# A tail rearranged in a fused top-k attention and MLP kernel: PE turns, a thinner MLP stretch, three products on GpSimd

## The chip, the cores and the metric

One core of one Trainium2 chip. The metric is the device time in microseconds (us) of one execution. Engines: PE (matmul), DVE (vector), ACT (scalar), POOL (GpSimd), SP (issues DMAs).

## What is computed

```python
scores = q @ k.T / 8                       # 8 batches x 8 heads, 576 x 576, head width 64
mask   = scores >= 32nd largest of the row
attn   = softmax of the masked scores
x      = (attn @ v), heads side by side    # 4608 x 512
h      = x @ w_in                          # 512 x 2048
out    = (max(h, 0) + alpha * min(h, 0)) @ w_out   # 4608 x 512
```

## The kernel before

**Tiles and ticks.** Two heads make a pair (32 pairs, `NPAIR`); a pair's score rows are nine tiles of 128 rows: tiles j = 0 to 7 are row chunk j // 2 of the head j % 2, and tile 8 holds the last 64 rows of both heads. The 288 tiles (`NT`) run in the list `ORDER`, one a tick of the loop at line 875. Every engine's order of work is written out by that loop; inside a tick, PE, ACT, DVE and POOL each get the steps of different tiles. `put(tick, slot, f)` files a step for a later tick, and `run(tick, slot)` issues what was filed. The slots "act", "pe", "dve", "dvx" and "end" stand at fixed places of the tick.

**One tile.** PE makes scores (`scores`, L333), ACT copies them with a bias (`act_b`, L342), sums their signs (`act_s`, L348) and takes the exponential (`act_e`, L353). POOL makes a sign word SG of the sum (`side_of`, L358), DVE flips the tile with it (`flip`, y, L364). One tick later DVE takes the eight largest of six segments (`seg_ops`, L374), then merges them (`merge_ops`, L389 and L391); every third tile the limit KP of the row is picked (L402 to L418). Seven ticks after the scores (`LAG_W`) the weights are made, in one of two ways: for tiles below `NW = NT - 6`, DVE makes a 0/1 mask (`mask`, L438, one buffer `mk`) and POOL multiplies it with the exponential (`weights`, L448); for the last six, DVE does both in one instruction (L445), at tick 289 for three and 292 for three. Each two tiles of a pair and chunk share a buffer `w2`, and SP issues a transposing DMA of it into `wT` (L461).

**The last batch.** The last four pairs, 28 to 31 (`LAST`, from `P0`), run chunk by chunk, so that a chunk's 128 output rows are ready for the MLP early. `tail_of` files for each chunk i and half g (two pairs): `av_last(i, g)` on PE (weights times v, 20 matmuls, L499, into `pu`), `rz_last` and `out_last` on DVE (reciprocal L568, scaled copy into `xb`, L575), `x_turn` (transposing DMA of `xb` into `xT`, L585) and the MLP block of these rows. For chunk three `turn_last` turns the rows with PE against an identity (L597) and copies them with DVE (L598).

**MLP.** `mlp_steps` gives a block's steps into a list `back`: ph steps (hidden rows, 16 matmuls of 128 columns, L725, followed by an ACT relu into gT, L731) and three pz steps (20 matmuls of 512 columns in parts of 7, 7 and 6, L739 and L743, followed by an ACT copy to o_sb, L748, and an output DMA). A block of 128 rows has four ph and three pz steps. Each tick the loop pops steps from `back` while `credit` (line 905) is above 0: 1.9 is added a tick, 2.4 from tick 288 on; a ph step costs 0.9, a pz part 1.5. Up to tick 253 one step a tick is popped, from tick 254 (`N0 + 2`) on as many as the credit allows. The ACT part of a popped step is issued at the start of the next tick. Matmul results of the MLP go to two PSUM banks in turn, from tick 288 on to the two score banks.

**The end.** `flush` empties `back`. Then `av_last(3, 1)`, `rz_last`, `out_last`, `last_ph(0)` (half of the hidden sums of chunk three, L611), `turn_last(1)`, `last_ph(1)` and `last_pz` (two halves of 256 columns, L628 and L631, copied by ACT and DVE, L634). `check_group` and `checks` (L466, L478 to L482) are sums over all tiles that end in a flag (`final_flag`, L486 and L487; `read_flag`), after which a slow general path is run or skipped; they are filed for ticks 292 to 297.

Of the kernel before, what the change touches and what calls it, by code (L numbers as in the profile page):

```python
# [32 lines left out]
def kernel(  # L33
# [406 lines left out]
    def weights(n, fused):  # L440
        p, j = ORDER[n]
        d, t = pairs[p], tiles.pop(n)
        dst = w_dst(n)
        if fused:
            nc.vector.scalar_tensor_tensor(out=dst, in0=t["b"], scalar=row_limit(n),  # L445
                                           in1=t["e"], op0=ALU.is_ge, op1=ALU.mult)
        else:
            nc.gpsimd.tensor_tensor(dst, t["mk"], t["e"], ALU.mult)  # L448
        if j == 8:
            d["wTm"] = prep.tile([128, 9, 128], BF16, name="wT", bufs=6)  # L450
            if fused:
                nc.vector.tensor_copy(d["wm"][:, S:640], d["wm"][:, 0:64])
            else:
                nc.gpsimd.tensor_tensor(d["wm"][:, S:640], t["mk"][:, 0:64], t["e"][:, 0:64],
                                        ALU.mult)
            nc.sync.dma_start_transpose(d["wTm"][:, 0:5, :], d["wm"])
            nc.sync.dma_start_transpose(d["wTm"][:, 5:9, :], d["wm"][:, 64:S])
        elif j % 2 == 1:
            wT = prep.tile([128, 9, 128], BF16, name="wT", bufs=6)
            d["wT", j // 2] = wT  # L460
            nc.sync.dma_start_transpose(wT, d["w2"])  # L461

    xb, xm = {}, {}

# [87 lines left out]

    pul = {}

    def av_last(i, g):
        x_tiles(B - 1)
        m = 128 if i < 4 else 64
        pul[i, g] = pu = ps_d.tile([128, 4, V1], FP32, name="pu", tag="pd")
        for s in range(2):
            d = pairs[P0 + 2 * g + s]  # L560
            for side in range(2):
                cs = slice(0, 128) if i < 4 else slice(64 * side, 64 * side + 64)
                av_one(pu[0:m, 2 * s + side, :], d, d["wT", i] if i < 4 else d["wTm"], side, cs)

    def rz_last(i, g):
        m = 128 if i < 4 else 64
        rz = attn.tile([128, 6], FP32, name="rz", bufs=4)
        nc.vector.reciprocal(rz[0:m, 0:4], pul[i, g][0:m, :, D])  # L568
        pul[i, g] = pul[i, g], rz

    def out_last(i, g):
        m = 128 if i < 4 else 64
        pu, rz = pul.pop((i, g))
        dst = xb[B - 1][i] if i < 4 else xm[B - 1]
        nc.vector.tensor_tensor(  # L575
            dst[:, 256 * g:256 * g + 256].rearrange("p (s d) -> p s d", s=4), pu[0:m, :, 0:D],
            rz[0:m, 0:4].unsqueeze(2).to_broadcast([m, 4, D]), ALU.mult)
# [11 lines left out]
    t7 = 7 * S  # L589
    CL = t7 % NX + 64 + 384  # L590

    def turn_last(h):
        pool, tag = (ps_a, "pa") if h == 0 else (ps_m, "misc")
        xa = pool.tile([128, 2, 128], BF16, name="xa", tag=tag)
        for j in range(2):
            c0 = 128 * (2 * h + j)
            nc.tensor.transpose(xa[:, j, :], xb[B - 1][3][:, c0:c0 + 128], ident_b)  # L597
        nc.vector.tensor_copy(xT[:, 2 * h:2 * h + 2, CL:CL + 128], xa)  # L598

    lastc = {}  # L600

# [17 lines left out]
                        lastc["ph"][u // 2][:, u % 2, :].rearrange("p (f t) -> p f t", f=4),  # L619
                        AF.Relu)  # L620

    def last_pz():
        o0 = t7 + 384
        for h, (pool, tag) in enumerate(((ps_a, "pa"), (ps_m, "misc"))):
            cs = slice(256 * h, 256 * h + 256)
            pz = pool.tile([128, 256], FP32, name="pz", tag=tag)
            for kk in range(NKT):
                nc.tensor.matmul(pz, xT[:, kk, CL:CL + 128], w_id_b[:, kk, cs], start=(kk == 0),  # L628
                                 stop=False)
            for f in range(NFT):  # L630
                nc.tensor.matmul(pz, lastc["g"][:, f, 0:128], w_out_b[:, f, cs], start=False,  # L631
                                 stop=(f == NFT - 1))
            o_sb = mlp.tile([128, DM], FP32, name="o_sb", tag="stage", bufs=3)
            (nc.scalar.copy if h == 0 else nc.vector.tensor_copy)(o_sb[:, 0:256], pz)  # L634
            nc.sync.dma_start(out[o0:o0 + 128, cs], o_sb[:, 0:256])

    def weight_steps():
        hold = {}
# [133 lines left out]

    PE_TICK = 1.9
    LAG_S, LAG_M, LAG_W = 2, 3, 7
    NW = NT - 6

    E = mybir.EngineType
    with tc.manual_schedule(engines={E.PE, E.Activation, E.DVE, E.Pool, E.SP}):
        cal = {}

        def put(tick, eng, f):
            cal.setdefault((tick, eng), []).append(f)

        def run(tick, eng):
            for f in cal.pop((tick, eng), ()):
                f()
# [8 lines left out]
            while blocks and blocks[0][0] + blocks[0][1] <= lim:  # L795
                back.extend(mlp_steps(*blocks.pop(0)))

        def flush():
            while back:
                pe_f, act_f, _, takes = back.popleft()  # L800
                if takes and len(after) >= 2:
                    after.popleft()()
                pe_f()
                if act_f:
                    after.append(act_f)
            while after:
                after.popleft()()

        def tail_of(n, wn):
            wp, wj = ORDER[wn]  # L810
            b = wp // KPB
            if wp in (PA, PA + 1):
                if (wj == 8 or wj % 2) and wp == PA + 1:
                    i = wj // 2
                    put(n + 3, "pe", lambda: av_alt(i))
                    put(n + 4, "dve", lambda: rz_alt(i))
                    put(n + 6, "act", lambda: out_alt(i))
                    put(n + 6, "end", lambda: x_turn(b, (i,)))
                    if i in (1, 3, 4):
                        lim = (b + 1) * S if i == 4 else b * S + 128 * i + 128  # L820
                        put(n + 9, "end", lambda: feed(lim))
            elif wp < P0:
                if wj == 3:
                    put(n + 3, "pe", lambda: av(wp, 0))
                    put(n + 4, "dve", lambda: av_rz(wp, 0))
                    put(n + 6, "act", lambda: av_out(wp, 0))
                    if wp % KPB == KPB - 1 and b >= 5:
                        put(n + 6, "end", lambda: x_turn(b, (0, 1)))
                        put(n + 8, "end", lambda: feed(b * S + 256))
                if wj == 8:  # L830
                    put(n + 4, "pe", lambda: av(wp, 1))
                    put(n + 5, "dve", lambda: av_rz(wp, 1))
                    put(n + 7, "act", lambda: av_out(wp, 1))
                    if wp % KPB == KPB - 1:
                        put(n + 7, "end", lambda: x_turn(b, range(2 if b >= 5 else 0, 5)))
                        put(n + 9, "end", lambda: feed((b + 1) * S))
            elif (wj == 8 or wj % 2) and wp % 2:
                i, g = wj // 2, (wp - P0) // 2
                dt = 2
                if i == 3 and g == 1:  # L840
                    put(n + dt, "pe", flush)
                put(n + dt, "pe", lambda: av_last(i, g))
                where = "end" if i == 3 and g == 0 else "dvx"
                put(n + dt + 1, where if where == "end" else "dve", lambda: rz_last(i, g))
                put(n + dt + 1, where, lambda: out_last(i, g))
                if i == 3:
                    if g == 1:
                        put(n + dt + 1, where, lambda: last_ph(0))
                    put(n + dt + 2 - g, where, lambda: turn_last(g))
                    if g == 1:  # L850
                        put(n + dt + 1, where, lambda: (last_ph(1), last_pz()))
                elif g == 1:
                    put(n + dt + 1, "dvx", lambda: x_turn(b, (i,)))
                    put(n + dt + 2, "end", lambda: back.extend(mlp_steps(*last.pop(i))))

# [19 lines left out]
        while n < end or back or after:  # L875
# [26 lines left out]
            if n >= 3 and n % 3 == 0 and n - 3 < NT:  # L902
                sel_a((n - 3) // 3)
            nb = 1 if n < N0 + 2 else 2
            credit = min(credit, 0.0) + (2.4 if n >= NT else 1.9)
            first = True
            while back and credit > 0.0 and (first or nb == 2):
                pe_f, act_f, cost, takes = back[0]
# [31 lines left out]
            for i in range(max(len(segs), len(merges), 2)):  # L940
                if i < len(segs):
                    segs[i]()
                if i < len(merges):
                    merges[i]()
            run(n, "dve")
            if 0 <= lm < NT and lm % 3 == 0:
                limit(lm // 3)
            if pick and n < NT:
# [4 lines left out]
            if pick:  # L953
                sel_pr(mn // 3)
                held = [lambda m=mn // 3: sel_sum(m)]
                if mn % TPP == TPP - 1:
                    put(n + 2, "dve" if mn < NT - 1 else "end", lambda g=mn // TPP: check_group(g))
                    if mn == NT - 1:
                        put(n + 2, "end", checks)
                        put(n + 3, "end", final_flag)  # L960
                        put(n + 7, "end", read_flag)
            run(n, "end")
            n += 1
        assert not cal and not blocks and not last
# [138 lines left out]
```

## Time and profile before

| what | value |
|---|---|
| median of three runs | 877.69 us (875.2 to 878.11) |
| profiled execution | 876.05 us |
| its span, first to last instruction | 873.9 us |
| mean granted TensorE clock | 0.925 |
| last DVE copy ends | 867.79 us |

Times inside the profile count from the span's start. Rows of the time order give start, duration, engine, line, operation, out <- in, the count that was merged, and in brackets the idle time before it with what ended it. Rows of the waits give the total, the number and the longest. Rows of the stretches give each engine's busy time with the count of its instructions, the granted clock, the DMA engines' share and GB/s.

### The profile page before, as it was taken

Reading aid. Unit: us, or ns where it says so; the run is one execution under the profiler, and the core shown is the slowest. Engines: PE = TensorE matmul, PEld = TensorE weight load, DVE = VectorE, ACT = ScalarE, POOL = GpSimd, SP = SyncE. Lnnn points to the kernel's source line nnn. Section 1 sums busy time; section 2 is a strip of 40 time slices with the busy share of each in tenths; the row PEclk is TensorE's granted clock in tenths of the full one; section 3 lists DMA queues with packets and bytes.
Section 4 is the critical chain, followed back from the end, with each engine's and each line's share of the span. In section 5 each row is a group of like instructions: output and inputs, shape, how many; then the busy total and the mean of one; then the engine's idle time right before and its main releaser. Section 6 shows DMA issues by size and latency. Waiting matters only on the chain. (4 is left out here: it accounts for less than half of the span.)

```text
span 873.9 us, 20604 instructions
## 1 busy us (share of the span) xinstructions
PE 715.2 (82%) x5698; PEld 425.6 (49%) x5771; DVE 834.9 (96%) x5187; ACT 789.7 (90%) x1872; POOL 430.3 (49%) x630
## 2 busy tenths in 40 slices
PE   5675698778968799777988789978897878999976
PEld 3443344334544345444454445644455555665655
DVE  4999999999999999999999999999999999899991
ACT  6999999989999999889999989999999998899841
POOL 1455445555555555555554545555555555455520
PEclk9568779889999999999997989999999999999989
DMA  7899645644665445564476446575455535444441
GB/s 161 159 171 211 120 90 89 129 90 95 134 144 109 101 108 113 103 135 94 108 158 123 85 97 130 108 135 96 96 123 120 120 71 124 92 90 97 77 95 45
DMA packets 342619, 99.37 MB, mean 114 GB/s; under 512 B 334672, under 2 KB 334944, under 8 KB 342496
## 3 DMA queue, kind: packets, MB, share of 16 engines
q1 hardware_dynamic: 340144, 95.58, 54.1%
q0 software_dynamic: 1152, 2.10, 1.8%
q8 instruction: 47, 0.77, 0.4%
q14 instruction: 76, 0.62, 0.2%
q10 hardware_dynamic: 1200, 0.30, 0.2%
HBM read 36.71 MB, written 9.44 MB: 53 GB/s over the span
## 5 line engine op out<-in xcount | busy, mean ns | idle before, releaser
L448 POOL TENSOR_TENSOR w<-mk,e 128x576 bf16<-128x576 bf16 x250 | 318.8, 1275 | 337.7 <-DVE mk L438 185.6
L374 DVE MAX8 C<-y 128x8 f32<-128x96 f32 x1728 | 418.4, 242 | 0.1
L333 PE MATMUL ps<-qkT 64*128 64x288 f32 (+1 forms) x1280 | 250.0, 468 | 28.3 <-ACT b L342 27.7
L348 ACT ACTIVATE h<-b 128x576 bf16<-128x576 f32 x288 | 203.5, 706 | 1.5
L342 ACT ACTIVATE b<-ps,NT 128x576 f32<-128x576 f32 x288 | 201.9, 760 | 1.9 <-PE ps L333 1.9
L725 PE MATMUL ph<-xT,w_in_b 128*128 128x128 bf16 (+2 forms) x997 | 151.2, 295 | 51.1 <-ACT gT L731 37.2
L353 ACT ACTIVATE e<-b 128x1152 bf16<-128x1152 f32 (+1 forms) x157 | 174.0, 1109 | 2.4 <-POOL w L448 2.3
L333 PEld LDWEIGHTS ps<-qkT 64*128 64x128 f32 (+1 forms) x1280 | 130.6, 192 | 89.5 <-ACT b L342 52.0
L389 DVE MAX8 L<-C 128x8 f32<-128x48 f32 x864 | 162.3, 188 | 0.1
L364 DVE TENSOR_SCALAR y<-b,SG 128x576 int32<-128x576 int32 x288 | 146.8, 510 | 9.0 <-POOL SG L358 8.5
L438 DVE TENSOR_SCALAR mk<-b,KP 128x576 bf16<-128x576 f32 x282 | 143.5, 509 | 0.0
L725 PEld LDWEIGHTS <-w_in_b 128*128 128x128 bf16 x1024 | 83.0, 102 | 113.1 <-issue 89.7
L743 PE MATMUL pz<-w_out_b,gT 128*128 128x512 bf16 x544 | 132.1, 380 | 1.1 <-issue 0.5
L731 ACT ACTIVATE gT<-ph 128x512 bf16<-128x512 f32 x140 | 85.9, 623 | 33.7 <-PE ph L725 33.5
L391 DVE MATCH_REPLACE8 C<-L,C 128x48 f32<-128x48 f32 x576 | 108.1, 188 | 0.0
L743 PEld LDWEIGHTS <-gT 128*128 128x128 bf16 x560 | 51.7, 98 | 68.4 <-issue 13.4
L499 PE MATMUL pu<-v_bf,wT 128*128 128x65 bf16 (+1 forms) x1600 | 68.6, 197 | 14.3 <-DMA wT<-w 7.3
L499 PEld LDWEIGHTS <-wT 128*128 128x128 bf16 (+1 forms) x1600 | 64.3, 102 | 25.7 <-DMA wT<-w 7.7
L358 POOL TENSOR_SCALAR SG<-S_all 128x1 int32<-128x1 f32 x288 | 64.7, 225 | 18.8 <-ACT h L348 18.8
L448 POOL TENSOR_TENSOR wm<-mk,e 128x576 bf16<-128x576 bf16 x32 | 40.8, 1275 | 50.3 <-DVE mk L438 46.2
L348 ACT ACTIVATION_READ_ACCUMULATOR h<-b 128x1 f32 x288 | 63.3, 220 | 0.0
L528 ACT ACTIVATE xb<-pu,rz 128x64 bf16<-128x64 f32 x208 | 50.6, 370 | 0.0
(116 smaller groups left out, 729.0 us busy)
## 6 DMA issues: line engine op xcount, KB each, us to landing
out_dram<-o_sb SPq DMA_DIRECT2D x34, 256.0 KB, 2.4
st_q<-in_q_dram SPq DMA_DIRECT2D x64, 128.0 KB, 2.9
st_v<-in_v_dram SPq DMA_DIRECT2D x64, 128.0 KB, 2.6
kst<-in_k_dram SPq DMA_DIRECT2D x62, 128.0 KB, 2.7
w_stage<-in_moe_w_out_dram SPq DMA_DIRECT2D x16, 256.0 KB, 3.1
w_in_b<-in_moe_w_in_dram POOLq DMA_DIRECT2D x8, 256.0 KB, 6.2
wT<-w SPq DMA_TRANSPOSE x128, 3.3
st_q<-in_q_dram SPq DMA_DIRECT2D x32, 32.0 KB, 2.5
```

What stands on the lines that cost most here:

```text
L333: nc.tensor.matmul(o_, l_, r_, start=True, stop=True)
L342: nc.scalar.activation(t["b"].rearrange("p (a c) -> p a c", a=2), t["ps"], AF.Identity, bias=NT0[:, p * TPP + j:p * TPP + j + 1], scale=ON ...
L348: nc.scalar.activation(h, tiles[n]["b"], AF.Sign, accum_out=S_all[:, n:n + 1])
L353: nc.scalar.activation(e, tiles[n0]["bu"], AF.Exp, scale=scl)
L364: nc.vector.tensor_scalar(t["y"].bitcast(I32), t["b"].bitcast(I32), FLIP, SG[:, n:n + 1], ALU.bitwise_xor, ALU.bitwise_xor)
L374: return [lambda g=g: nc.vector.max(out=C[:, n % TPP, g, :], in_=t["y"][:, g * SEG:(g + 1) * SEG]) for g in range(NSEG)]
L389: ops.append(lambda r=r, src=src: nc.vector.max(out=L[:, 8 * r:8 * r + 8], in_=src))
L438: nc.vector.tensor_scalar(t["mk"], t["b"], row_limit(n), None, ALU.is_ge)
L448: nc.gpsimd.tensor_tensor(dst, t["mk"], t["e"], ALU.mult)
L499: nc.tensor.matmul(o_, wT[:, 4 * side + c, cs], d["v"][:, 5 * side + c, :], start=(c == 0), stop=(c == 4))
L725: nc.tensor.matmul(hold[f][:, i, :], w_in_b[:, kk, (f + i) * 128:(f + i + 1) * 128], xT[:, kk, c0:c0 + tb], start=(kk == 0), stop=(kk == N ...
L743: nc.tensor.matmul(pz[0:m], hold["gT"][:, f, r0:r0 + m], w_out_b[:, f, :], start=False, stop=(f == NFT - 1))
```

## The change

- **Weights by PE.** For pair 31's chunk two and for chunk three of pairs 30 and 31 (`BY_PE`), the transposing DMA is left out. `w_turn` turns the nine 128-column blocks of `w2` with PE transposes in two parts (four and five), and ACT copies each part into `wT`. For chunk two it is issued in tick 287.
- **Chunk two's rows by PE.** `x_turn` of chunk two is left out. In tick 288, in a new slot "mid" (after DVE's merges, before KP and y), stand `rz_last(2, 1)`, `out_last(2, 1)`, four PE transposes and one ACT copy into `xT`, and the MLP block is filed there, in tick 288 instead of 290.
- **Less MLP work a tick.** From tick 254 to 265 the credit is 1.2 a tick instead of 1.9.
- **Three products on GpSimd.** `NW` is `NT - 3`: the tiles 282, 283 and 284 get mask and POOL product in ticks 289, 290 and 291; the last three stay with DVE in tick 292.
- **The finale** is one function in tick 292. It empties `back` down to two steps, turns weights, empties it to one, turns the rest, then runs `av_last(3, 1)` pair by pair with the turn of the first two 128-column blocks of chunk three's rows between, the last step of `back`, and the end as before.
- **Checks behind outputs.** `check_group` and `checks` are issued after `last_ph(1)`, `final_flag` after the first half of `last_pz`, `read_flag` after the second.

```diff
-        elif j % 2 == 1:
+        elif j % 2 == 1 and (p, j // 2) not in BY_PE:
...
+    BY_PE = ((NPAIR - 1, 2), (NPAIR - 2, 3), (NPAIR - 1, 3))
+
+    def w_turn(p, i, part):
+        d = pairs[p]
+        if part == 0:
+            d["wT", i] = prep.tile([128, 9, 128], BF16, name="wT", bufs=6)
+        cs = range(4 * part, 4 + 5 * part)
+        if i == 2:
+            pool, tag = ps_d, "pd"
+        else:
+            pool, tag = ((ps_a, "pa"), (ps_m, "misc"))[part]
+        wt = pool.tile([128, len(cs), 128], BF16, name="wt", tag=tag)
+        for c in cs:
+            nc.tensor.transpose(wt[:, c - cs[0], :], d["w2"][:, 128 * c:128 * c + 128], ident_b)
+        nc.scalar.copy(d["wT", i][:, cs[0]:cs[-1] + 1, :], wt)
...
-    NW = NT - 6
+    NW = NT - 3
...
-        def flush():
-            while back:
+        def flush(keep):
+            while len(back) > keep:
...
+        def finale():
+            pA, pB = NPAIR - 2, NPAIR - 1
+            flush(2)
+            w_turn(pA, 3, 0)
+            w_turn(pA, 3, 1)
+            w_turn(pB, 3, 0)
+            flush(1)
+            w_turn(pB, 3, 1)
+            rz_last(3, 0)
+            out_last(3, 0)
+            av_last(3, 1, (0,))
+            turn_pe(3, 0, 2, nc.scalar.copy)
+            av_last(3, 1, (1,))
+            rz_last(3, 1)
+            out_last(3, 1)
+            flush(0)
+            last_ph(0)
+            turn_pe(3, 2, 4, nc.vector.tensor_copy)
+            last_ph(1)
+            check_group(NPAIR - 1)
+            checks()
+            last_pz((final_flag, read_flag))
...
+                if (i, g) == (2, 1):
+                    put(n + 1, "pe", lambda: (w_turn(wp, i, 0), w_turn(wp, i, 1)))
+                    put(n + dt, "mid", lambda: (rz_last(i, g), out_last(i, g)))
+                    put(n + dt, "mid", lambda: turn_pe(i, 0, NKT, nc.scalar.copy))
+                    put(n + dt, "mid", lambda: back.extend(mlp_steps(*last.pop(i))))
+                    return
...
-            credit = min(credit, 0.0) + (2.4 if n >= NT else 1.9)
+            credit = min(credit, 0.0) + (2.4 if n >= NT else 1.2 if nb == 2 and n < N0 + 14 else 1.9)
```

More of the change, by code (lines that the diff above doesn't have):

```diff
@@ L553, with av_last @@
     pul = {}
-    def av_last(i, g):
+    def av_last(i, g, ss=range(2)):
         x_tiles(B - 1)
         m = 128 if i < 4 else 64
-        pul[i, g] = pu = ps_d.tile([128, 4, V1], FP32, name="pu", tag="pd")
-        for s in range(2):
+        if ss[0] == 0:
+            pul[i, g] = ps_d.tile([128, 4, V1], FP32, name="pu", tag="pd")
+        pu = pul[i, g]
+        for s in ss:
             d = pairs[P0 + 2 * g + s]
@@ L590, with turn_pe @@
     CL = t7 % NX + 64 + 384
[L592 to L598, printed above, removed]
+    def turn_pe(i, k0, k1, copy):
+        c0 = t7 % NX + 64 + 128 * i
+        pool, tag = (ps_a, "pa") if k0 == 0 else (ps_m, "misc")
+        xa = pool.tile([128, k1 - k0, 128], BF16, name="xa", tag=tag)
+        for k_ in range(k0, k1):
+            nc.tensor.transpose(xa[:, k_ - k0, :], xb[B - 1][i][:, 128 * k_:128 * k_ + 128],
+                                ident_b)
+        copy(xT[:, k0:k1, c0:c0 + 128], xa)
     lastc = {}
@@ L620, in last_ph, with last_pz @@
                         AF.Relu)
-    def last_pz():
+    def last_pz(between):
         o0 = t7 + 384
@@ L635, in last_pz @@
             nc.sync.dma_start(out[o0:o0 + 128, cs], o_sb[:, 0:256])
+            between[h]()
     def weight_steps():
@@ L839, in tail_of @@
                 dt = 2
-                if i == 3 and g == 1:
-                    put(n + dt, "pe", flush)
+                if (i, g) == (3, 1):
+                    finale()
+                    return
                 put(n + dt, "pe", lambda: av_last(i, g))
-                where = "end" if i == 3 and g == 0 else "dvx"
-                put(n + dt + 1, where if where == "end" else "dve", lambda: rz_last(i, g))
-                put(n + dt + 1, where, lambda: out_last(i, g))
                 if i == 3:
[L847 to L852, printed above, removed]
+                    return
+                if (i, g) == (2, 1):
[3 more added lines that the diff above has]
+                    put(n + dt, "mid", lambda: back.extend(mlp_steps(*last.pop(i))))
+                    return
+                put(n + dt + 1, "dve", lambda: rz_last(i, g))
+                put(n + dt + 1, "dvx", lambda: out_last(i, g))
+                if g == 1:
                     put(n + dt + 1, "dvx", lambda: x_turn(b, (i,)))
@@ L945 @@
             run(n, "dve")
+            run(n, "mid")
             if 0 <= lm < NT and lm % 3 == 0:
@@ L955 @@
                 held = [lambda m=mn // 3: sel_sum(m)]
[L956 to L961, printed above, removed]
+                if mn % TPP == TPP - 1 and mn < NT - 1:
+                    put(n + 2, "dve", lambda g=mn // TPP: check_group(g))
             run(n, "end")
```

## The prediction, before the changed kernel ran

> **What bounds the kernel now.** I read the page first, then the stretches of the last sixth, the waits there, and the time order of the end. All times are microseconds of the profiled execution, measured from its span's start.
>
> ```profile
> PE 715.2 (82%) x5698; PEld 425.6 (49%) x5771; DVE 834.9 (96%) x5187; ACT 789.7 (90%) x1872; POOL 430.3 (49%) x630
> ```
>
> DVE bounds the program, so an edit elsewhere counts only where DVE stands still. All edits lie behind tick 254, so I cut the rest of the span into stretches (PE, PEld, DVE, ACT, POOL busy; granted clock; DMA):
>
> ```profile
> 740.00:777.50 37.50, 35.30 (x331) 23.59 (x332) 34.28 (x212) 31.58 (x75) 18.53 (x27) 0.96 0.45 88
> 777.50:842.90 65.40, 60.46 (x583) 40.26 (x588) 65.14 (x394) 56.53 (x112) 34.54 (x49) 1.00 0.44 86
> 842.90:846.34 3.44, 0.00 (x1) 0.00 (x1) 3.44 (x15) 0.00 (x0) 0.00 (x0) 0.85 0.87 204
> 846.34:867.80 21.46, 20.50 (x233) 17.23 (x233) 8.88 (x37) 5.41 (x10) 0.00 (x0) 0.87 0.27 60
> 867.80:873.90 6.10, 0.00 (x0) 0.00 (x0) 0.00 (x0) 0.00 (x0) 0.00 (x0) 0.89 0.09 31
> ```
>
> DVE is idle for 3.22 in the first stretch, full in the second, and from 846.34 on PE is the bound: 20.50 of 21.46. The waits say why (us in total, times, longest; windows 740 to 845 for DVE, 735 to 785 for ACT, 740 to 874 for PE):
>
> ```profile
> DVE y L364 <- POOL SG L358: 2.7, 3, 1.8
> DVE rz L542 <- PE pu L499: 0.3, 1, 0.3
> ```
> ```profile
> ACT o_sb L748 <- PE pz L743: 4.2, 2, 3.4
> ```
> ```profile
> PE ph L725 <- DMA xT<-xb: 5.5, 2, 4.7
> ```
>
> The three stalls of `flip` are a chain: ACT stood 3.4 for the third part of an MLP product, so its sign sums came late, so SG, so `y`. The 4.7 of PE is chunk two's transposing DMA: the back list had run dry in ticks 289 and 290.
>
> **Less MLP work in ticks 254 to 265.** By the order of the instructions of both kernels: before, ticks 256 and 257 pop pz pz and pz, and the copy of that product stands ahead of tick 258's score copies on ACT. After, the same ticks pop ph and pz, and the copy stands at tick 260. Two product steps, about 3.0 by the rates below, lie ahead of the scores no more; the ACT wait was 3.4. I let all 3.0 of DVE stalls go (2.7 + 0.3; bounds 2.0 and 3.2). The price: five steps (two ph, three pz) pass behind tick 289. Ticks 266 to 287 pop 17 ph and 18 pz in place of 20 and 14. With the rates of the next fence (0.94 and 1.44) that is 3.0 more PE work in the second stretch, where PE had 65.40 - 60.46 = 4.9 idle. It fits, barely; the bound above is a new DVE stall of 1.5, as tick 275 now holds two pz besides its scores.
>
> **The end, walked through in the old time frame.** First the rates, from a part where PE ran at full clock:
>
> ```profile
> 820.00 3.75 PE L725 MATMUL ph<-xT,w_in_b 128*128 128x128 bf16 x64
> ...
> 825.24 1.02 PE L739 MATMUL pz<-w_id_b,xT 128*128 128x512 bf16 x3
> ...
> 829.56 0.80 PE L499 MATMUL pu<-v_bf,wT 128*128 128x65 bf16 x20
> 830.29 1.24 PE L333 MATMUL ps<-qkT 64*128 64x288 f32 x8
> ...
> 840.83 0.80 PE L499 MATMUL pu<-v_bf,wT 128*128 128x65 bf16 x20
> 846.34 3.57 PE L725 MATMUL ph<-xT,w_in_b 128*128 128x128 bf16 x32 [4.71 <-DMA xT<-xb]
> 849.70 1.30 PE L499 MATMUL pu<-v_bf,wT 128*128 128x65 bf16 x20
> 850.82 2.57 PE L725 MATMUL ph<-xT,w_in_b 128*128 128x128 bf16 x32
> 853.23 1.03 PE L739 MATMUL pz<-w_id_b,xT 128*128 128x512 bf16 x3
> ```
>
> A ph step of 16 takes 3.75 / 4 = 0.94; a product of 20 takes 829.56 - 825.24 = 4.32, so 1.51, 1.51 and 1.30 in its parts; a pu of 20 takes 0.73. A PE transpose has the shape of a ph matmul, so 0.06 each.
>
> Now DVE, ACT and POOL around it:
>
> ```profile
> 839.68 0.51 DVE L438 TENSOR_SCALAR mk<-b,KP 128x576 bf16<-128x576 f32 x1
> ...
> 841.89 0.14 DVE L418 SCALAR_TENSOR_TENSOR KP<-KK,SG 128x3 int32<-128x3 int32 x1
> ...
> 842.38 0.17 DVE L568 RECIPROCAL rz<-pu 128x4 f32<-128x4 f32 x1
> 842.59 0.42 DVE L575 TENSOR_TENSOR xb<-pu,rz 128x256 bf16<-128x256 f32 x1
> 842.93 2.27 DVE L445 SCALAR_TENSOR_TENSOR w<-b,KP,e 128x576 bf16<-128x576 f32 x3
> ...
> 848.97 2.28 DVE L445 SCALAR_TENSOR_TENSOR w<-b,KP,e 128x576 bf16<-128x576 f32 x3
> ```
> ```profile
> 834.97 1.09 ACT L731 ACTIVATE gT<-ph 128x512 bf16<-128x512 f32 x2
> ```
> ```profile
> 749.41 0.71 ACT L208 CAST v_bf<-st_v 128x640 bf16<-128x640 f32 x1
> ```
> ```profile
> 840.28 1.27 POOL L448 TENSOR_TENSOR w<-mk,e 128x576 bf16<-128x576 bf16 x1 [1.26 <-DVE mk L438]
> ```
>
> *Three products on GpSimd.* Three fused products (2.27) become three masks. Each mask takes about 0.45 of DVE's time (0.51, overlapped), so DVE is done some 0.9 earlier, near 850.3 instead of 851.25. One `mk` buffer makes each mask wait for POOL's 1.27, but at least 1.7 of other DVE work lies between them. This gain I cost at nothing: PE, not DVE, sets the end. If PE were early it would be worth its 0.9.
>
> *Chunk two by PE.* `rz_last(2, 1)` and `out_last` now run ahead of KP and `y`: from 841.89, done 842.01 + 0.51 = 842.52 (843.01 before). PE, which has done two ph and pu by about 841, waits for them. Then the last two transposes (0.2 with the hand-over), the ACT copy (half of 1.09: 0.5), and behind it on ACT the relu of the first ph (0.5), which PE's third ph needs for its bank: PE goes on at 843.8 instead of 846.34. So PE still stands some 1.3 to 2 ahead of `xb` and 1.1 behind it; the transposing DMA is out of the way. The first nine weight transposes, of pair 31's chunk two, sit in that slack and cost nothing; without it they would cost 0.55.
>
> *From 843.8, in program order on PE:* two ph 1.9, a product 4.3 (850.0); three ph 2.8, pu 0.7, a ph 0.9 (854.5); part one of the last block's product 1.5 (856.0); nine transposes 0.55, then 0.3 of waiting for the first ACT copy, four transposes 0.25 (857.1); part two 1.5, five transposes 0.3 (858.9); half of pu, two row transposes, the rest of pu after ACT's 640-wide copy 0.95 (859.85); part three 1.3 (861.15); `last_ph(0)` 1.8 (862.95). The rest is the old end:
>
> ```profile
> 860.30 0.28 PE L597 MATMUL xa<-ident_b,xb 128*128 128x128 bf16 x2
> ```
> ```profile
> 860.62 0.29 DVE L598 COPY xT<-xa 128x256 bf16<-128x256 bf16 x1 [1.26 <-PE xa L597]
> ```
> ```profile
> 860.96 1.95 PE L611 MATMUL ph<-xT,w_in_b 128*128 128x128 bf16 x32 [0.38 <-DVE xT L598]
> ```
> ```profile
> 867.37 0.42 DVE L634 COPY o_sb<-pz 128x256 f32<-128x256 f32 x1 [6.46 <-PE pz L631]
> ```
>
> ```profile
> wT<-w SPq DMA_TRANSPOSE x128, 3.3
> ```
>
> From 860.30 to 867.79 are 7.5, so after ends at 870.4 in the old frame against 867.8: **2.6 later**. It does 7.7 more PE work behind 843.8 (two ph, a product, weight turns with their waits 1.5); it starts 2.5 earlier and is spared the slow rows above (3.57, 1.30 and 2.57 for 1.9, 0.7 and 1.9). Weights of chunk three by PE save no wait here: DVE is done at 850.3, and a transposing DMA, 3.3 from issue to landing, would be there before PE asks at 856. They cost about 1.4 (bounds 0 and 2.6: a pair of transposes reads 0.28).
>
> *Checks behind outputs* move some 2.4 of DVE work under `last_ph(1)` and the products, where DVE has 6.46 idle: nothing, both ways. The 6.1 after the last copy stay.
>
> **The clock** is what I cannot walk through. Windows of 3.41, on the grid on which the granted clock changes:
>
> ```profile
> 736.07:739.49 3.42, 1.38 (x11) 0.76 (x10) 3.42 (x21) 3.39 (x8) 1.65 (x3) 1.00 0.98 159
> 739.49:742.90 3.41, 3.41 (x35) 3.35 (x32) 3.41 (x20) 2.06 (x7) 1.47 (x2) 0.50 0.24 71
> 804.34:807.75 3.41, 2.42 (x32) 1.55 (x28) 3.41 (x23) 3.41 (x8) 1.75 (x3) 1.00 0.52 142
> 841.89:845.30 3.41, 0.00 (x0) 0.00 (x0) 3.38 (x10) 0.00 (x0) 0.00 (x0) 1.00 0.79 189
> 845.30:848.71 3.41, 2.37 (x23) 2.37 (x23) 3.20 (x23) 0.41 (x1) 0.00 (x0) 0.50 0.54 102
> 848.71:852.13 3.42, 3.42 (x45) 3.42 (x43) 3.31 (x9) 0.78 (x2) 0.00 (x0) 0.50 0.35 66
> ```
>
> A window with PE busy 1.38 of 3.42 was followed by half clock; one with 2.42 was not. After has 2.4 to 3.1 of PE idle within some 3.5: most likely one window falls to half, which costs half of 3.41, 1.7 (bounds 0 and 3.4). The Trainium skill, "TensorE: Matmul & The Clock Gate", section "Part 1: The HAM clock gate", lets the clock fall only after at least one idle window of about 3.4 us. By that rule the clock holds here and the sum is 1.7 less; the trace speaks against it (1.38 busy was enough to fall), so it is a rival.
>
> **The sum.** -3.0 (stalls) + 2.6 (end) + 1.7 (clock) = +1.3. The profiled execution took 876.05 (span 873.9 and 2.15 around it), so 877.35 against it. It lies 1.64 below the median shown, 877.69; on that scale the forecast is **879.0**, no change that a measurement of this kernel can tell (about 0.3%, 2.6 us, so 875.1 to 880.3).
>
> **Rivals.**
> - *The clock holds*, because the wait is shared by two windows that each stay busy enough: -0.4, 877.3. For it: 2.42 busy held. Against: the row of 1.38. The Trainium skill's rule named above gives the same time.
> - *Slower: the half clock stays a second window.* Place: the two windows behind chunk two's wait. The rows of 845.30 and 848.71 show it after 2.37 busy at half clock. Another 1.7: 880.7. It decides when the PE wait straddles a window's edge, so that the first slow window is itself part idle. With a new stall of 1.5 from the fuller ticks it is 882.2.
> - *Faster: the end is shorter than walked.* The clock holds, 3.2 of stalls go, and the weight turns fit into waits that my walk doesn't have (ACT's relus ahead of PE in the finale), so their 1.4 cost nothing and the 0.9 of GpSimd counts: -3.2 + 2.6 - 1.4 - 0.9 = -2.9, 874.8. For it: the design of the finale, which only pays if PE gets there when DVE does. Against: PE's 20.50 of 21.46.
> - *The change doesn't do what it says:* ACT is late in ticks 254 to 265 all the same, since two row-8 score groups fall there, and only 2.0 of stalls go: 880.0.
>
> **How the numbers follow.** Forecast 0.29, clock holds 0.14, too few stalls removed 0.04: together 0.47 within 0.3%. Second slow window 0.25 and with new stalls 0.10: 0.35 slower by more. Shorter end: 0.18 faster by more. The range leaves out the outer half of the faster case and the worst of the slower one: 874.3 to 882.5.
>
> **What would show it.** Right: DVE without SG waits between 740 and 780 and everything there 3 earlier; the wait of ph for the DMA gone, one for ACT's relu of 1 in its place; PE busy through to the end; weight transposes far behind DVE's last product. Wrong: SG waits left or new ones after tick 266 (step one); PE waiting for DVE's last products in the finale, which would make the GpSimd edit count (step of the walk); the clock at full, or at half for over 3.41, behind chunk two.

## The result and the profile after

In paired runs the changed kernel took 879.49 us (median of 22, 876.16 to 882.03) and the kernel before 876.38 (22, 874.83 to 881.31). The ratio of these runs is 1.0027, 95% interval 1.0015 to 1.004: about 2.4 us slower (1.3 to 3.5; the medians alone stand 3.1 apart). That is inside the 0.3% that the prediction calls no change, but close to its edge of 2.6, and with so many runs the interval tells it from zero. The profiled execution took 878.3 us (span 876.4, granted clock 0.912) against 876.05 (873.9, 0.925).

The whole-span line of the page answers little: PE has 5.8 more, DVE the same.

```profile
PE 721.0 (82%) x5728; PEld 428.9 (49%) x5802; DVE 834.8 (95%) x5186; ACT 793.9 (91%) x1880; POOL 434.9 (50%) x633
```

The same stretches as before say more (PE, PEld, DVE, ACT, POOL busy; granted clock; DMA), with the end cut at DVE's last copy:

```profile
740.00:777.50 37.50, 33.95 (x326) 22.96 (x327) 36.90 (x228) 35.47 (x86) 20.01 (x30) 0.95 0.52 91
777.50:842.90 65.40, 59.45 (x570) 38.91 (x574) 65.14 (x394) 54.08 (x108) 34.31 (x48) 0.99 0.39 85
...
846.34:870.00 23.66, 22.08 (x265) 16.86 (x265) 6.83 (x22) 8.63 (x16) 0.43 (x1) 1.00 0.13 39
```

The first stretch shows the gain: DVE is busy 36.90 where it was busy 34.28. The third shows the loss: from 846.34 PE works 22.08, where it worked 20.50. The waits name both (DVE 740 to 845; PE 735 to 876):

```profile
DVE P L251 <- PE pr L243: 0.4, 1, 0.4
```
```profile
PE xa L615 <- DVE xb L593: 2.8, 1, 2.8
PE ph L745 <- ACT gT L751: 2.8, 4, 1.2
```

No SG wait is left on DVE (a new wait of 0.4, for PE's `pr`, is), and the 4.7 of `ph` for the DMA is gone. In its place the PE transposes of chunk two's rows wait 2.8 for DVE's `xb`, and the ph step behind them, the third of its block, 1.2 for ACT's relu. PE's time order (L615 row transposes, L745 ph, L759 and L763 pz, L476 weight transposes):

```profile
836.64 0.81 PE L515 MATMUL pu<-v_bf,wT 128*128 128x65 bf16 x20
837.28 0.27 PE L615 MATMUL xa<-ident_b,xb 128*128 128x128 bf16 x2
840.35 0.29 PE L615 MATMUL xa<-ident_b,xb 128*128 128x128 bf16 x2 [2.80 <-DVE xb L593]
841.81 3.33 PE L745 MATMUL ph<-xT,w_in_b 128*128 128x128 bf16 x32 [1.17 <-ACT gT L751]
...
855.03 0.67 PE L476 MATMUL wt<-ident_b,w 128*128 128x128 bf16 x9
856.09 0.38 PE L476 MATMUL wt<-ident_b,w 128*128 128x128 bf16 x4 [0.40 <-ACT wT L477]
```

The wait of 1.17 comes about in the same way, on ACT. ACT waited for the turned rows, while the relus of two ph steps that PE had finished at 836.8 came behind them in its program:

```profile
840.68 0.59 ACT L617 COPY xT<-xa 128x512 bf16<-128x512 bf16 x1 [3.72 <-PE xa L615]
```

After the wait the 32 ph matmuls take 3.33, where full clock takes 1.95. The windows of the clock's grid show why: PE was busy 0.29 of one, and the next ran at half.

```profile
837.92:841.33 3.41, 0.29 (x2) 0.17 (x3) 3.38 (x22) 0.65 (x2) 1.46 (x2) 1.00 0.57 123
841.33:844.75 3.42, 2.94 (x28) 2.94 (x28) 3.25 (x23) 1.52 (x3) 2.55 (x2) 0.50 0.24 45
844.75:848.16 3.41, 3.36 (x20) 1.70 (x20) 3.34 (x6) 0.60 (x1) 1.27 (x1) 1.00 0.46 89
```

DVE, in time order, with the anchors used below (mask of tick 288, `xb` of chunk two, the last fused products, the last copy):

```profile
837.45 0.52 DVE L438 TENSOR_SCALAR mk<-b,KP 128x576 bf16<-128x576 f32 x1
...
839.87 0.42 DVE L593 TENSOR_TENSOR xb<-pu,rz 128x256 bf16<-128x256 f32 x1
...
845.52 1.26 DVE L418 SCALAR_TENSOR_TENSOR KP<-KK,SG 128x3 int32<-128x3 int32 x1
846.82 2.27 DVE L445 SCALAR_TENSOR_TENSOR w<-b,KP,e 128x576 bf16<-128x576 f32 x3
...
859.45 0.18 DVE L586 RECIPROCAL rz<-pu 128x4 f32<-128x4 f32 x1 [5.98 <-PE pu L515]
...
869.62 0.42 DVE L653 COPY o_sb<-pz 128x256 f32<-128x256 f32 x1 [2.20 <-PE pz L650]
```

The two spans compare as follows. The mask of tick 288 comes 2.23 earlier (839.68 to 837.45), the last copy ends 32.59 behind it in place of 28.11, 4.48 more, and 6.36 follow in place of 6.11. Together 2.5, the difference of the spans.

### The profile page after: what moved, and what is told of

Same layout as the page of the kernel before. It is cut to its first block, busy times and chain, and to the rows that moved or that the text cites. A ratio compares the mean times of both kernels' runs of the same rounds, so it can differ in the third digit from the quotient of the medians.

```text
span 876.4 us, 20675 instructions
## 1 busy us (share of the span) xinstructions
PE 721.0 (82%) x5728; PEld 428.9 (49%) x5802; DVE 834.8 (95%) x5186; ACT 793.9 (91%) x1880; POOL 434.9 (50%) x633
## 5 line engine op out<-in xcount | busy, mean ns | idle before, releaser
L448 POOL TENSOR_TENSOR w<-mk,e 128x576 bf16<-128x576 bf16 x253 | 323.1, 1277 | 338.9 <-DVE mk L438 178.8
L374 DVE MAX8 C<-y 128x8 f32<-128x96 f32 x1728 | 421.0, 244 | 0.1
L745 PE MATMUL ph<-xT,w_in_b 128*128 128x128 bf16 (+2 forms) x997 | 152.6, 295 | 45.8 <-ACT gT L751 37.4
L438 DVE TENSOR_SCALAR mk<-b,KP 128x576 bf16<-128x576 f32 x285 | 145.3, 510 | 0.0
L745 PEld LDWEIGHTS <-w_in_b 128*128 128x128 bf16 x1024 | 81.8, 101 | 109.3 <-issue 85.9
L763 PE MATMUL pz<-w_out_b,gT 128*128 128x512 bf16 x543 | 132.1, 380 | 1.2 <-issue 0.5
L763 PEld LDWEIGHTS <-gT 128*128 128x128 bf16 x560 | 51.7, 98 | 68.0 <-issue 13.3
L515 PE MATMUL pu<-v_bf,wT 128*128 128x65 bf16 (+1 forms) x1600 | 70.8, 200 | 14.7 <-DMA wT<-w 8.9
L515 PEld LDWEIGHTS <-wT 128*128 128x128 bf16 (+1 forms) x1600 | 66.1, 104 | 25.5 <-DMA wT<-w 9.5
```

The source lines that it names most:

```text
L374: return [lambda g=g: nc.vector.max(out=C[:, n % TPP, g, :], in_=t["y"][:, g * SEG:(g + 1) * SEG]) for g in range(NSEG)]
L438: nc.vector.tensor_scalar(t["mk"], t["b"], row_limit(n), None, ALU.is_ge)
L515: nc.tensor.matmul(o_, wT[:, 4 * side + c, cs], d["v"][:, 5 * side + c, :], start=(c == 0), stop=(c == 4))
L745: nc.tensor.matmul(hold[f][:, i, :], w_in_b[:, kk, (f + i) * 128:(f + i + 1) * 128], xT[:, kk, c0:c0 + tb], start=(kk == 0), stop=(kk == N ...
L763: nc.tensor.matmul(pz[0:m], hold["gT"][:, f, r0:r0 + m], w_out_b[:, f, :], start=False, stop=(f == NFT - 1))
```

## The experiments

**Theory:** PE sets the end from chunk two on, and two edits that each pay spoil one another. The 1.2 credit frees DVE, but pushes MLP steps behind tick 289; the row turns of chunk two stand in PE's program ahead of these steps, so PE waits for `xb` with runnable work queued behind. **Rivals:** the weight turns of chunk three are the loss, the GpSimd edit is, or the clock alone. Each ratio is to runs of the kernel before that were made beside it (medians 876.11 to 877.44). A figure in us behind a ratio is a difference of ratios times 876.4. The last column is a length inside one profiled execution, from the start of DVE's `xb` of chunk two to the start of its last copy: it leaves out what happened earlier. `xb` itself stands 0.5 earlier where PE turns chunk two's rows (2.42 behind the mask of tick 288 in after, 2.91 in before), so compare this length among before, e1, e6 and e7, or among the others.

| kernel | median us | ratio to before, 95% | profile: `xb` to last copy |
|---|---|---|---|
| before | 876.38 | 1 | 24.8 |
| after | 879.49 | 1.0027 (1.0015 to 1.004) | 29.75 |
| e1: before, credit edit alone | 872.18 | 0.9944 (0.9932 to 0.9957) | 23.9 |
| e2: after, rows turned two ticks later | 874.23 | 0.9967 (0.9946 to 0.9988) | 25.4 |
| e3: after, chunk three's weights by DMA | 877.37 | 1.0005 (0.9992 to 1.0018) | 27.8 |
| e4: after, credit 1.9 again | 874.1 | 0.9974 (0.9962 to 0.9985) | 22.2 |
| e5: after, six fused products again | 879.7 | 1.0032 (1.0016 to 1.0048) | 30.6 |
| e6: e1 and checks behind outputs | 871.89 | 0.9945 (0.9923 to 0.9966) | 22.8 |
| e7: e6 and three products on GpSimd | 872.39 | 0.9954 (0.9934 to 0.9974) | 23.9 |
| e8: after, PE kept busy in the wait | 877.43 | 1.0006 (0.9989 to 1.0024) | 28.4 |
| e9: e2 and e3 together | 873.16 | 0.9959 (0.9939 to 0.9979) | 24.4 |

### e1: the credit edit alone

```diff
 (before)
-            credit = min(credit, 0.0) + (2.4 if n >= NT else 1.9)
+            credit = min(credit, 0.0) + (2.4 if n >= NT else 1.2 if nb == 2 and n < N0 + 14 else 1.9)
```

> The kernel before with one edit: credit 1.2 in ticks 254 to 265. Theory (PE paces the end; after loses by PE's wait for xb, the half clock behind it and the weight turns): the SG stalls of 740 to 780 go (2.7 less), the five deferred steps fill PE's 4.7 wait for the transposing DMA down to about 1, and no window falls to half clock: 4 to 5 us less than before, ratio about 0.995. Rival (the deferred MLP steps themselves make the end late, wherever the turns are made): the deferred 6.3 us of PE work come back at the end and eat the stalls: ratio 0.998 to 1.003.

It measured 0.9944, 4.9 us faster (3.8 to 6.0), as the theory had it. DVE's waits (740 to 845), then PE's time order in e1:

```profile
DVE P L251 <- PE pr L243: 0.6, 1, 0.6
```
```profile
837.61 1.95 PE L725 MATMUL ph<-xT,w_in_b 128*128 128x128 bf16 x32
839.39 1.03 PE L739 MATMUL pz<-w_id_b,xT 128*128 128x512 bf16 x4
840.25 3.62 PE L743 MATMUL pz<-w_out_b,gT 128*128 128x512 bf16 x16
...
851.86 0.19 PE L486 MATMUL ptot<-ones_f,tot 128*1 128x1 f32 x2 [1.42 <-DVE junkg L482]
```

The stalls are gone, and the steps pushed back run from 837.6 to 843.9, where before PE stood 4.71 for chunk two's transposing DMA. So the edit pays at both ends: the late steps fill a DMA wait, and the ph matmuls run at full clock (1.95, against 3.57 in before). Between these two profiled executions the spans differ by 3.1 (873.9 and 870.8), 2.2 of it ahead of `xb`; for the rest, e1's profiled execution (873.02) is 0.8 above e1's median, and that of before (876.05) 1.4 below the median that before had beside e1 (877.44).

### e2: chunk two's rows turned two ticks later

```diff
 (after)
-                    put(n + dt, "mid", lambda: turn_pe(i, 0, NKT, nc.scalar.copy))
-                    put(n + dt, "mid", lambda: back.extend(mlp_steps(*last.pop(i))))
+                    put(n + dt + 2, "pe", lambda: turn_pe(i, 0, NKT, nc.scalar.copy))
+                    put(n + dt + 2, "pe", lambda: back.extend(mlp_steps(*last.pop(i))))
```

> The changed kernel with one edit: chunk two's row turn and its MLP block are issued on PE two ticks later (290), behind the product of the block before it. Theory: PE no longer waits for xb (2.8) nor for the relu behind the row copy on ACT (1.2), no window falls to half clock (1.4): 5 us less than after, about 2.5 less than before, ratio to before 0.997. Rival (the end waits for DVE's last products and the weights): at most 1 us less than after, ratio 1.002.

It measured 0.9967, 5.3 less than after. PE in e2:

```profile
837.45 0.80 PE L515 MATMUL pu<-v_bf,wT 128*128 128x65 bf16 x20
838.31 1.95 PE L745 MATMUL ph<-xT,w_in_b 128*128 128x128 bf16 x32
840.09 1.03 PE L759 MATMUL pz<-w_id_b,xT 128*128 128x512 bf16 x4
840.96 2.32 PE L763 MATMUL pz<-w_out_b,gT 128*128 128x512 bf16 x10
843.11 0.39 PE L615 MATMUL xa<-ident_b,xb 128*128 128x128 bf16 x4
...
848.74 0.49 PE L515 MATMUL pu<-v_bf,wT 128*128 128x65 bf16 x10 [0.94 <-DMA wT<-w]
```

It is the same work in another order: two ph and most of a product fill the time until `xb` is there, and the transposes (843.11) wait for nothing. The account agrees: the two waits and the half clock, 2.80 + 1.17 + (3.33 - 1.95), less the new 0.94, are 4.4; `xb` to last copy went from 29.75 to 25.4. The traces and the times agree that this is the main cause: where the turns stand in PE's program.

### e3: chunk three's weights by the transposing DMA

```diff
 (after)
-    BY_PE = ((NPAIR - 1, 2), (NPAIR - 2, 3), (NPAIR - 1, 3))
+    BY_PE = ((NPAIR - 1, 2),)
...
-            w_turn(pA, 3, 0)
-            w_turn(pA, 3, 1)
-            w_turn(pB, 3, 0)
             flush(1)
-            w_turn(pB, 3, 1)
```

> The changed kernel with chunk three's weights (pairs 30 and 31) turned by the transposing DMA again; chunk two's by PE as in after. Theory: PE is spared 18 transposes and two waits for ACT's copies, 1.6 to 1.8 us less than after, ratio to before about 1.001. Rival (PE turns save the landing of the DMA): the same as after or up to 2 us more, ratio 1.003 to 1.005.

It measured 1.0005, 1.9 less than after. PE in e3:

```profile
842.12 0.28 PE L615 MATMUL xa<-ident_b,xb 128*128 128x128 bf16 x2 [2.80 <-DVE xb L593]
843.57 3.35 PE L745 MATMUL ph<-xT,w_in_b 128*128 128x128 bf16 x32 [1.17 <-ACT gT L751]
...
858.32 0.48 PE L515 MATMUL pu<-v_bf,wT 128*128 128x65 bf16 x10
```

The wait for `xb` and the half clock are as in after, and `pu` at 858.32 waits for no DMA. The 18 weight transposes and their waits for ACT cost 1.9 and save nothing here. They are a second cost, the smaller one.

### e4: the credit at 1.9 again, all else as in after

```diff
 (after)
-            credit = min(credit, 0.0) + (2.4 if n >= NT else 1.2 if nb == 2 and n < N0 + 14 else 1.9)
+            credit = min(credit, 0.0) + (2.4 if n >= NT else 1.9)
```

> The changed kernel with credit 1.9 in ticks 254 to 265 as before. Theory: the SG stalls (2.7) come back, but five MLP steps less lie behind chunk two's turn, 6.3 us of PE work; PE waits for xb and, in the finale, up to 1.5 for DVE's last products: 2 to 4 us less than after, ratio to before 0.998 to 1.000. Rival (less MLP work is the edit that pays): 2.7 more than after, ratio 1.005.

It measured 0.9974, 4.6 less than after where 2 to 4 were expected. So the edit that gains 4.9 on the kernel before costs 4.6 in the changed one (1.0027 - 0.9974), and the rest of the change without it is 2.3 faster than before (1.3 to 3.3). DVE's waits (740 to 845) and PE's time order in e4:

```profile
DVE y L364 <- POOL SG L358: 2.7, 3, 1.8
```
```profile
842.00 0.80 PE L515 MATMUL pu<-v_bf,wT 128*128 128x65 bf16 x20
842.64 0.27 PE L615 MATMUL xa<-ident_b,xb 128*128 128x128 bf16 x2
843.53 0.29 PE L615 MATMUL xa<-ident_b,xb 128*128 128x128 bf16 x2 [0.62 <-DVE xb L593]
844.49 3.75 PE L745 MATMUL ph<-xT,w_in_b 128*128 128x128 bf16 x64 [0.67 <-ACT xT L617]
```

The 2.7 of stalls are back, yet the end is 7.5 shorter (22.2 for 29.75): the MLP steps are done by 842, so PE reaches the transposes when `xb` is nearly there, and one block instead of one and a half lies behind them.

### e5: six fused products again

```diff
 (after)
-    NW = NT - 3
+    NW = NT - 6
```

> The changed kernel with the last six products on DVE again (NW = NT - 6). Theory: DVE is done some 6 us before PE asks for the last weights, so its 0.9 is worth nothing: within 0.5 us of after, ratio to before 1.002 to 1.003. Rival (the three products on GpSimd make DVE's last stretch late, KP took 1.26 beside POOL's product where it takes 0.14 alone): 1 us less than after, ratio 1.0015.

It measured 1.0032 against 1.0027, no difference that the times can tell. PE, then DVE, in e5:

```profile
839.54 0.39 PE L615 MATMUL xa<-ident_b,xb 128*128 128x128 bf16 x2 [2.80 <-DVE xb L593]
841.10 3.57 PE L745 MATMUL ph<-xT,w_in_b 128*128 128x128 bf16 x32 [1.17 <-ACT gT L751]
...
845.32 0.68 PE L759 MATMUL pz<-w_id_b,xT 128*128 128x512 bf16 x2 [0.22 <-issue]
```
```profile
839.05 0.42 DVE L593 TENSOR_TENSOR xb<-pu,rz 128x256 bf16<-128x256 f32 x1
...
845.93 2.28 DVE L445 SCALAR_TENSOR_TENSOR w<-b,KP,e 128x576 bf16<-128x576 f32 x3
```

From `xb` to the end of the last products it is 9.2 here (839.05 to 848.21) and 9.2 in after (839.87 to 849.09). Three products on GpSimd do not free DVE at all: the 0.9 they save is what KP's 1.26 takes back (0.16 in e5), of which more below.

The length in the table, 30.6 for 29.75, is the clock. The wait for `xb` is the same 2.80, but in this execution the clock's windows begin at 838.66 and 842.07, and the wait lies across an edge. PE was busy 1.49 in the window up to 838.66 and 1.36 in the next, and both windows from 838.66 to 845.48 were granted 0.50. PE's 16 pz matmuls (L763) start 0.8 later behind `xb` than in after, and from there to the last copy both take 23.8.

### e6 and e7: the cheaper edits on top of e1

```diff
 (before with e1's line: e6)
-    def last_pz():
+    def last_pz(between):
...
+            between[h]()
...
-                        put(n + dt + 1, where, lambda: (last_ph(1), last_pz()))
+                        put(n + dt + 1, where, lambda: (last_ph(1), check_group(NPAIR - 1),
+                                                          checks(), last_pz((final_flag, read_flag))))
...
-                if mn % TPP == TPP - 1:
-                    put(n + 2, "dve" if mn < NT - 1 else "end", lambda g=mn // TPP: check_group(g))
-                    if mn == NT - 1:
-                        put(n + 2, "end", checks)
-                        put(n + 3, "end", final_flag)
-                        put(n + 7, "end", read_flag)
+                if mn % TPP == TPP - 1 and mn < NT - 1:
+                    put(n + 2, "dve", lambda g=mn // TPP: check_group(g))
 (e7 as well)
-    NW = NT - 6
+    NW = NT - 3
```

> The kernel before with credit 1.2 in ticks 254 to 265, and the checks, the flag's sum and its reading behind last_ph(1) and the outputs as in after. Theory: with the thinner stretch alone PE waited 1.4 for the checks' sum in the middle of the last block's product; that wait goes: 1.4 us less than with the thinner stretch alone, ratio to before 0.993. Rival (PE's wait there only moves to the weights of the last rows): ratio 0.9945.

> The kernel of e6 with three more products on GpSimd (NW = NT - 3). Theory: PE asks for pair 29's chunk three about when its transposing DMA lands (0.6 of waiting in the thinner stretch alone); that product now ends about 2 later on POOL, so PE waits more there: 0.5 to 1.5 us more than e6, ratio 0.994 to 0.995. Rival (DVE is the pace again once PE is early, so its 0.9 counts): 0.9 less than e6, ratio 0.992.

They measured 0.9945 and 0.9954; beside e1's 0.9944 the times separate none of the three. One profiled execution of each shows differences of a microsecond (that of e7 took 876.46, 4.1 above its median). PE of e6 (its lines from L726 on are one further than before's), then of e7:

```profile
850.22 0.28 PE L597 MATMUL xa<-ident_b,xb 128*128 128x128 bf16 x2
850.33 2.97 PE L744 MATMUL pz<-w_out_b,gT 128*128 128x512 bf16 x13
```
```profile
851.54 0.49 PE L499 MATMUL pu<-v_bf,wT 128*128 128x65 bf16 x10 [1.10 <-DMA wT<-w]
```

In e6 the product follows without the 1.42 that e1's PE waited for the sums of the flag; PE waits 0.28 for weights later (853.90), and the end is 1.1 shorter. In e7 it is 1.1 longer again. Of that, 0.6 is the wait for weights, 1.10 where e6 waits 0.50 (845.70). That the masks and products spread over ticks 289 to 291 bring these weights later is likely, but not shown.

### e8: the wait filled with idle work

```diff
 (after)
-        for k_ in range(k0, k1):
+        busy = [0, 1] * 24 if i == 2 else []
+        for k_ in [*busy, *range(k0, k1)]:
             nc.tensor.transpose(xa[:, k_ - k0, :], ...
```

The 48 added transposes write the first two blocks again and again, with their own values.

> The changed kernel with 48 more PE transposes of the first two column blocks of chunk two's rows (into the places that are written again with the same values), so that PE works 2.7 us of its 2.8 wait for xb. Theory: no window falls to half clock, the two ph behind it take 1.9 instead of 3.3: 1.4 us less than after, ratio to before 1.001. Rival (the rule that only a whole idle window slows the clock, and the two ph are slow for another reason): the same as after, ratio 1.0027.

It measured 1.0006, 1.8 less than after. PE in e8 (ph is L746 here), and the stretch around it:

```profile
838.15 3.36 PE L616 MATMUL xa<-ident_b,xb 128*128 128x128 bf16 x52
842.69 1.95 PE L746 MATMUL ph<-xT,w_in_b 128*128 128x128 bf16 x32 [1.17 <-ACT gT L752]
```
```profile
840.50:843.90 3.40, 2.10 (x35) 1.81 (x33) 3.37 (x20) 1.70 (x4) 1.28 (x1) 1.00 0.47 89
```

PE goes on at the same moment (1.94 after `xb` starts, as in after) but at full clock: ph takes 1.95, and the end is 1.4 shorter, just 3.33 - 1.95. So this is the price of one window at half clock, and it is about a quarter of the 5.35 that the waits and the clock make together (2.80, 1.17 and 1.38), not the whole.

### e9: e2 and e3 together

The edit is the two diffs above.

> The changed kernel with both single undoings together: chunk two's rows turned in tick 290 and chunk three's weights by the transposing DMA. Theory that the loss behind the wait (2.8 + 1.2, half clock) and the weight turns (1.9 by the run that left them out) are two separate costs on one engine: PE sets the end, so they add: 5.3 less than the changed kernel by the ratios (0.9967 for the late turn, 1.0005 for the weights by DMA, 1.0027 for the change), 0.9945, the time of the credit edit alone. Rival, that the two hide in one another (with PE undisturbed, the transposing DMAs land after PE asks, a new wait of 1 to 2 for wT): 0.9965 or more, no better than the late turn alone.

It measured 0.9959 (0.9939 to 0.9979), between the two: the times leave it open. PE in e9:

```profile
850.82 0.49 PE L515 MATMUL pu<-v_bf,wT 128*128 128x65 bf16 x10 [0.94 <-DMA wT<-w]
...
855.67 0.49 PE L515 MATMUL pu<-v_bf,wT 128*128 128x65 bf16 x10 [0.44 <-DMA wT<-w]
...
856.46 0.49 PE L515 MATMUL pu<-v_bf,wT 128*128 128x65 bf16 x10 [0.18 <-DMA wT<-w]
```

The trace says that the two hide in one another in part. With PE no longer late, the DMA of chunk three's weights is waited for (0.44 and 0.18), and of e3's 1.9 about 1.0 is left (25.4 to 24.4). What weight turns by PE are worth hangs on how early PE is. The PE turns that e9 keeps, those of chunk two, show no gain over e7, which has none of them, though the two also end in different orders of steps: 0.9959 and 0.9954. The weight turns of chunk two were not tried by themselves.

## Why the prediction was right

The forecast was +1.3 for the span with no change within 0.3%; the profile shows +2.5, the paired runs +2.4. The steps held. The 1.2 by which the profile is above the forecast comes from four sizes, each below: 0.3 (stalls), 0.5 (the one execution), 0.2 (the wait) and 0.25 (behind the last copy).

- **Stalls of ticks 254 to 265, forecast -3.0.** They went as named. In size it is 2.7: the masks of tick 240 (L438), ahead of any edit, stand 0.5 later in the changed kernel's profiled execution, before and after in turn:

```profile
700.41 0.51 DVE L438 TENSOR_SCALAR mk<-b,KP 128x576 bf16<-128x576 f32 x1
```
```profile
700.89 0.51 DVE L438 TENSOR_SCALAR mk<-b,KP 128x576 bf16<-128x576 f32 x1
```

  So of the 2.23 at tick 288, 2.7 is the edit and -0.5 the one execution. The 0.4 of the new wait for `pr` is in it, which the prediction did not name. New stalls in the fuller ticks behind tick 266 did not come: DVE's 65.14 of 65.40 stayed.
- **The wait behind chunk two.** `xb` was done 2.84 behind the mask of tick 288, as walked. PE stood 2.80 for it, not 1.3 to 2, because it got there earlier; that by itself moved nothing behind it. PE was forecast to go on 4.1 behind that mask (843.8 - 839.68); it did after 4.4 (841.81 - 837.45). From there to the end of the last copy 26.6 and 1.7 of clock were walked, 28.3; it took 28.2. That this meets so closely is in part luck: the weight turns took 0.5 more, the clock 0.3 and the other rows 0.3 less. What the walk took as given, e2 shows to be the loss. The walk counted PE's standing for `xb`, but did not ask what could have run meanwhile, and so missed that an order of the same steps without the wait lay two ticks away.
- **Weight turns, forecast 1.4.** They took 1.9 (e3); the waits for ACT's copies (0.40 and 0.23) were larger than walked. That they save no wait held: DVE's last products end at 849.1, six before PE asks at 855.0.
- **The clock, forecast 1.7.** One window ran at half, as forecast, for 1.4 (e8). That it was one and not two is luck, as nothing in the prediction says where the edges fall. With the same wait of 2.80, after and e3 show one, and e5 shows two: the prediction's slower rival, under the condition that it named, a wait across a window's edge. In e5 the second window cost 0.8, not 1.7. The Trainium skill's rule ("TensorE: Matmul & The Clock Gate", "Part 1: The HAM clock gate": at least one idle window) is not settled by the window of 0.29, which was nearly idle; before's row of 1.38 busy, followed by half clock, stays against it, and so does e5's of 1.49.
- **GpSimd products, at nothing.** This was right (e5), for a second reason that the prediction lacked: DVE gains nothing (9.2 with and without), not 0.9.
- **Flag behind outputs, at nothing.** It is nothing in e6's times and 1.1 in its trace, by a wait (1.42) that the kernel before does not show.
- **The 6.1 behind the last copy** became 6.36.
- **Rivals.** In the changed kernel's profiled execution the clock did not hold, no second window fell, and more than 2.0 of stalls went. The shorter end did not come: PE was busy 22.08 of 23.66, the reason given against it.

Where it came near to failing is the sign of the parts. The prediction summed each edit's price; e1 and e4 show that the credit edit is worth -4.9 without the others and +4.6 with them, and the others -2.3 without it. Added up from these, the change would have been 7.2 faster. The sum came out right because it was walked through the program order of the changed kernel as a whole, not taken from the edits one by one.

The smallest ratio here is that of the kernel before with the credit edit alone (e1, 0.9944): 4.9 us faster than before, 7.3 than after. e6, e7 and e9 are not told from it.

## What to carry over

On an engine that runs its program in order, look at what stands behind a wait: replacing a slow transfer by work of the same engine can cost more than it saves if that work waits for its input with runnable steps queued behind it. Here issuing it two ticks later was worth 5.3 us. Two edits that each pay can spoil one another when both move work across the same wait, so try each alone and each left out. Idle time can be paid a second time: in these traces windows with PE busy 0.29, 1.38 and 1.49 of 3.41 were each followed by one at half clock, and one such window cost 1.4. The edges fell differently against the wait in different executions (837.92 in after, 838.66 in e5), so one trace does not settle how many windows a wait costs.

## What the runs showed of the hardware

- **A small DVE instruction lasted as long as a GpSimd product.** KP (L418, 128x3, two inputs in SBUF) takes 0.14 to 0.16 in before, where none of its 96 runs beside one of POOL's products. In after the last one takes 1.26, and POOL's product runs at the same time:

```profile
845.50 1.27 POOL L448 TENSOR_TENSOR w<-mk,e 128x576 bf16<-128x576 bf16 x1 [0.85 <-DVE KK L412]
```

  KP starts at 845.52 and ends at 846.78, POOL's product at 846.77. So it was in e2, e3, e4, e8 and e9 (1.26 to 1.27) and in e7 (1.20), the kernels with the GpSimd edit, and in none of those without (0.16 in e1, e5 and e6). The Trainium skill, "GPSIMD Engine Reference", section "8. Key points", says that GpSimd shares its SBUF interfaces with VectorE and names DVE instructions with two SBUF inputs; the rows agree, and show here a whole product's length of waiting. An instruction with one input was not slowed: MAX8 (L374) takes 0.24 in before, beside POOL's products (1317 times) as away from them (405). That the sharing is the cause was not tried by itself.
- **Transposes on PE keep the clock up.** e8 filled the wait with nothing else (52 in 3.36) and ran at 1.00 behind it, where after, with the same wait empty, fell to 0.50. The Trainium skill, "TensorE: Matmul & The Clock Gate", section "Part 4: PE-mode transpose", says that transposes do not count as busy in the same way; the run differs. The rows show them as matmuls with the identity, and do not show the mode that the page speaks of.
